# The start of a fused transformer block: the first weight matrix in half-width pieces, x tiles in another place among the loads

## The chip, the cores and the metric

The kernel runs on one core of a Trainium2 chip. The metric is device time in microseconds (us) of one execution. "Fast" runs are those that show no slow state. A ratio is the mean time of one kernel's fast runs over the mean of the other's fast runs of the same rounds, so it is not quite the ratio of the medians that are quoted.

Engines: PE is the tensor engine, PEld its weight loads, DVE the vector engine, ACT the scalar engine, POOL GpSimd, SP the sync engine, whose queue issues most DMAs. "LN1" is the first layer norm. A load "lands" when its data are in on-chip memory; it then counts up a semaphore, on which the reader waits. "Eviction" is the copy of a finished sum out of PSUM, the memory that PE writes to.

## The reference, cut to what matters

```python
# x: [1, 2048, 1024] bf16, D = 1024
h  = x + attention(layernorm(x) @ wqkv) @ wo     # sliding, dilated window of 8, 32 heads
h2 = h + mixer(layernorm(h))                     # gated MLP with a 2048 x 2048 token mix
```

Only the first step matters here: `layernorm(x) @ wq` for the first four tiles of 128 rows. `wq` is 1024 x 1024, 2 MB in bf16.

## The kernel before

PE runs 12 warm-up matmuls on zeros. Meanwhile the first loads are issued on two queues, SP (`dma`) and ACT (`A.dma_start`):

```python
csb = cpool.tile([P, 416], BF16, name="csb")        # identity and small constants
dma_w(csb[:], consts_d.ap()[:, :])                  # POOL queue
...
x_slot(0)
dma(xts[0][0:64, :], x2d[0:64, :])                  # x tile 0 in two row halves
A.dma_start(xts[0][64:P, :], x2d[64:P, :])
x_slot(1)
...
for q, kt in ((dma, 0), (A.dma_start, 1), (dma, 2), (A.dma_start, None), (dma, 4),
              (A.dma_start, 3), (dma, 5), (dma, 6), (dma, 7)):
    if kt is None:
        q(xts[1], x2d[P:2 * P, :])                  # x tile 1
    else:
        q(wsb[0][:, kt, :], wq_view[:, kt, 0:D])    # one row block of wq, 256 KB
load_x(2); load_x(3)
dma(wsb[1][:], ...)                                 # wk, 2 MB
... x tiles 4 to 7, then wv, 2 MB
```

LN1 of a tile is `stats` (DVE), a root (ACT), a reciprocal and a normalising pass (DVE). PE then transposes the tile and multiplies it:

```python
ln(0); xpose(0, xns[0], (0, 2)); xpose(0, xns[0], (2, 5))
for i in range(TPC):                                # four tiles
    acc = new_acc()
    for kt in range(KT):                            # eight row blocks
        if kt == 2 and i == 0:
            xpose(0, xns[0], (5, KT)); ln(1)
        if kt == QSPLIT and i + 1 < TPC:            # QSPLIT = 5
            xpose(i + 1, xns[i + 1], (0, 4), (4, KT))
        for nh in range(2):                         # two column halves
            T.matmul(acc[:, nh, :], xnT[...kt...], wsb[0][:, kt, nh * CH:(nh + 1) * CH], ...)
    if i + 2 < TPC:
        ln(i + 2)
    A.copy(qs0[:, i], acc...)                       # eviction on ACT
```

Much later one load matters for an experiment: `dma(bB[:], B_b_sp.unsqueeze(0).to_broadcast([P, S]))`, a bias for the last stage.

Of the kernel before, what the change touches and what calls it, by code (L numbers as in the profile page):

```python
# [18 lines left out]
S, D, H, DH, W_WIN, DIL = 2048, 1024, 32, 32, 8, 2  # L19
F, FH = 3584, 1792  # L20
P = 128
NT = S // P
CH = 512
NCH = S // CH
TPC = CH // P
KT = D // P
# [3 lines left out]
EPS = 1e-5  # L30
SCALE = DH ** -0.5
NEG = -1.0e9
NWARM = 12
XRB = 4
QSPLIT = 5
POOLLAT = 2.2
# [7 lines left out]
def _consts():  # L44
    c = np.zeros((P, 128 + 32 + 128 + 128), np.float32)
    c[:, 0:128] = np.eye(P)
    for p in range(P):
        c[p, 128 + p // 4] = 1.0
    for k in range(P):
        h = k % 32  # L50
        c[k, 160 + 4 * h:160 + 4 * h + 4] = 1.0
    for w in range(W_WIN):
        for s in range(16):
            if s - DIL * w < 0:
                c[0:32, 288 + w * 16 + s] = NEG
    return c.astype(ml_dtypes.bfloat16)
# [81 lines left out]
def kernel(  # L138
# [13 lines left out]
    V, A, T = nc.vector, nc.scalar, nc.tensor  # L152
    dma = nc.sync.dma_start
    dma_w = nc.gpsimd.dma_start
    x2d = A_x[0]
    out2d = out[0]

    consts_d = nc.inline_tensor(_consts(), name="qt_consts")
# [7 lines left out]

    cpool = ctx.enter_context(tc.tile_pool(name="consts", bufs=1))
    csb = cpool.tile([P, 416], BF16, name="csb")
    dma_w(csb[:], consts_d.ap()[:, :])
    ident = csb[:, 0:128]  # L170
    E32 = csb[:, 128:160]
    B4 = csb[:, 160:288]
# [10 lines left out]
    def wtile(shape, name, tag):  # L183
        return w16.tile(shape, BF16, name=name, tag=tag)
# [6 lines left out]
    def new_acc():  # L191
        return ps_acc.tile([P, 2, CH], FP32, name="acc", tag="acc")
# [9 lines left out]
    wq_view = A_wqkv.rearrange("(kt p) n -> p kt n", p=P)  # L202
    xnT = {}
    xts = {}
    pairs = {}

    def x_slot(i):
        if i // 2 not in pairs:
            pairs[i // 2] = l1.tile([P, 2, D], BF16, name="xp", tag="x4k", bufs=4)
        xts[i] = pairs[i // 2][:, i % 2, :]  # L210

    def load_x(i):
        x_slot(i)
        dma(xts[i], x2d[i * P:(i + 1) * P, :])
# [5 lines left out]
    wps = ps_att.tile([P, CH], FP32, name="wps", tag="L")  # L220
    for _ in range(NWARM):
        T.matmul(wps[:], warm[:, 0:P], warm[:], start=True, stop=True)

    x_slot(0)
    dma(xts[0][0:64, :], x2d[0:64, :])
    A.dma_start(xts[0][64:P, :], x2d[64:P, :])  # L226
    x_slot(1)
    wsb = [wtile([P, KT, D], "wq", "wA"), wtile([P, KT, D], "wk", "wA"), wtile([P, KT, D], "wv", "wB")]
    for q, kt in ((dma, 0), (A.dma_start, 1), (dma, 2), (A.dma_start, None), (dma, 4), (A.dma_start, 3), (dma, 5), (dma, 6), (dma, 7)):
        if kt is None:  # L230
            q(xts[1], x2d[P:2 * P, :])
        else:
            q(wsb[0][:, kt, :], wq_view[:, kt, 0:D])  # L233
    load_x(2)
    load_x(3)
    dma(wsb[1][:], wq_view[:, :, D:2 * D])
    for i in range(TPC, 2 * TPC):
        load_x(i)
# [2 lines left out]
    def stats(i):  # L241
        st = l1.tile([P, 2, 6], FP32, name="bnst", tag="bnst")
        V.bn_stats(st[:, 0, :], xts[i][:, 0:512])  # L243
        V.bn_stats(st[:, 1, :], xts[i][:, 512:1024])  # L244
        V.bn_aggr(mv1[:, i, :], st[:])

    def rstd_of(i):
        sd = l1.tile([P, 1], FP32, name="sd1", tag="sd1")
        A.activation(sd[:], mv1[:, i:i + 1, 1], ACTF.Sqrt, bias=eps_t[:])
        V.reciprocal(rstd1[:, i:i + 1], sd[:])  # L250

    def norm(i):
        xn = l1.tile([P, D], BF16, name="xn", tag="xn", bufs=4)
        for n0, n1 in ((0, 256), (256, 640), (640, D)) if i == 0 else ((0, D),):
            V.tensor_scalar(xn[:, n0:n1], xts[i][:, n0:n1], mv1[:, i, 0:1], rstd1[:, i:i + 1], op0=ALU.subtract, op1=ALU.mult)  # L255
        return xn
# [5 lines left out]
    def xpose(i, xn, *parts):  # L262
        for k0, k1 in parts:
            if i not in tps or k0 == 2:
                tps[i] = (ps_acc if i or k0 else ps_att).tile([P, KT, P], BF16, name="tpa" if i or k0 else "tp0", tag="acc" if i or k0 else "L")
            for a in range(k0, k1):
                T.transpose(tps[i][:, a, :], xn[:, a * P:(a + 1) * P], ident)  # L267
        for k0, k1 in parts:
            A.copy(xnT[0][:, k0:k1, i * P:(i + 1) * P], tps[i][:, k0:k1, :])
# [16 lines left out]
    with tc.manual_schedule(engines=manual):  # L286
        wsq = l1.tile([P, 1], FP32, name="wsq", tag="wsq")
        A.activation(wsq[:], eps_t[:], ACTF.Sqrt)
        xns = {}

        def ln(i):
            stats(i)
            rstd_of(i)
            xns[i] = norm(i)

        ln(0)
        xpose(0, xns[0], (0, 2))
        xpose(0, xns[0], (2, 5))
        for i in range(TPC):
            acc = new_acc()  # L300
            for kt in range(KT):
                if kt == 2 and i == 0:
                    xpose(0, xns[0], (5, KT))
                    ln(1)
                if kt == QSPLIT and i + 1 < TPC:
                    xpose(i + 1, xns[i + 1], (0, 4), (4, KT))
                for nh in range(2):
                    T.matmul(acc[:, nh, :], xnT[0][:, kt, i * P:(i + 1) * P], wsb[0][:, kt, nh * CH:(nh + 1) * CH],  # L308
                             start=(kt == 0), stop=(kt == KT - 1))
            if i + 2 < TPC:  # L310
                ln(i + 2)
            if i == 0:
                qs0 = att.tile([P, TPC, DLO, P], BF16, name="qs0", tag="oT")
            A.copy(qs0[:, i], acc[:].rearrange("p a b -> p (a b)").rearrange("p (m dl) -> p dl m", dl=DLO))
            nc.sync.dma_start_transpose(att_in[0][0][:, :, i * P:(i + 1) * P], qs0[:, i])
    wo_sb = wtile([P, DLO, D], "wo_sb", "wB")
    win_view = B_w_in.rearrange("(kt p) n -> p kt n", p=P)
# [537 lines left out]
    for c in range(NCH):  # L855
        wspT = wspTs[c]
        zg = p2.tile([P, NF, CH], BF16, name="zg", tag="zg")
        for fp in range(NF // 2):
            z1c = p2.tile([P, 2, CH], BF16, name="z1c", tag="z1c", bufs=8)
            dma(z1c[:], z1_d[2 * fp:2 * fp + 2, :, c * CH:(c + 1) * CH].rearrange("f p s -> p f s"))  # L860
            acc = new_acc()
            for j in range(2):
                f = 2 * fp + j
                for a in range(NT):
                    m_ = T.matmul(acc[:, j, :], z2sb[a][:, f * P:(f + 1) * P], wspT[:, a, :],  # L865
                                  start=(a == 0), stop=(a == NT - 1))
# [8 lines left out]
        for il in range(TPC):  # L875
            i = c * TPC + il
# [4 lines left out]
            for n0, n1 in cuts:  # L881
                acc = new_acc()[:].rearrange("p a b -> p (a b)")
                for f in range(NF):
                    wt, f0 = (wout_a, f) if f < 8 else (wout_b, f - 8)
                    for m0 in range(n0, n1, CH):
                        m1 = min(m0 + CH, n1)
                        T.matmul(acc[:, m0 - n0:m1 - n0], zg[:, f, il * P:(il + 1) * P], wt[:, f0, m0:m1],  # L887
                                 start=(f == 0), stop=(f == NF - 1))
# [29 lines left out]
```

## Time and profile before

| | before |
|---|---|
| median of the first three runs | 725.31 us (724.75 to 726.04) |
| span of the profiled execution | 723.8 us |
| PE busy | 714.0 us |
| transposes of x tile 2 start | 15.43 us |
| first matmul with wk | 24.52 us |

The page of the kernel before, parts 1 and 4: busy time by engine, and the chain of work that ended last, by engine.

```profile
PE 714.0 (99%) x3392; PEld 364.1 (50%) x3454; DVE 413.0 (57%) x435; ACT 238.2 (33%) x302; POOL 49.6 (7%) x57
...
PE 98%; DMA 1%; issue 0%; DVE 0%; ACTq 0%; ACT 0%
```

The profiled execution took 725.55 us (span 723.8).

PE is the limit everywhere but at the edges. The waits of PE over the whole run of the kernel before (who waited for whom: us in total, times, longest):

```profile
PE wps L222 <- DVE warm L219: 1.3, 1, 1.3
PE acc L308 <- DMA wq<-in_A_wqkv_dram: 1.1, 1, 1.1
PE tpa L267 <- DVE xn L255: 0.6, 1, 0.6
```

All three lie in the first 12 us. The timeline of PE there, kernel before: start, duration, line, operation, count, and in brackets the idle time before it with what ended it. L308 are the matmuls with wq, L267 the transposes, L396 the matmuls with wk.

```profile
7.16 1.04 PE L308 MATMUL acc<-wq,xnT 128*128 128x512 bf16 x4
...
8.20 0.59 PE L308 MATMUL acc<-wq,xnT 128*128 128x512 bf16 x2
9.86 1.02 PE L308 MATMUL acc<-wq,xnT 128*128 128x512 bf16 x4 [1.07 <-DMA wq<-in_A_wqkv_dram]
11.52 0.62 PE L267 MATMUL tpa<-csb,xn 128*128 128x128 bf16 x8 [0.63 <-DVE xn L255]
11.97 3.62 PE L308 MATMUL acc<-wq,xnT 128*128 128x512 bf16 x15
15.43 0.61 PE L267 MATMUL tpa<-csb,xn 128*128 128x128 bf16 x8
...
24.52 0.81 PE L396 MATMUL acc<-xnT,wk 128*128 128x512 bf16 x3
```

Up to 11.52 PE waits for a piece of wq, then for LN1 of x tile 1. From there it has no hole. So the start of tile 2's transposes (15.43) and of wk (24.52) are the marks for what the start is worth.

The loads under it, kernel before: issue, and the landing of the first and the last of the 16 parts of each load, one for each DMA engine. This table is made from the trace's landing records.

```
load              queue  issued  first part  last part
wq piece 0        SP      1.41      4.56       5.84
x tile 1          ACT     2.29      6.58       8.80
wq piece 3        ACT     2.76      8.37       9.82
wq piece 7 (last) SP      7.46     10.30      11.49
x tile 2          SP      7.83     10.96      12.15
```

Piece 3, on the ACT queue, landed after piece 4 on SP (9.13), though PE uses it first. Piece 7 was issued late: SP waited 2.2 us for a semaphore that an earlier load held until 7.44. The last parts of pieces 6 and 7 and of x tile 2 land 0.66 us apart (10.83, 11.49, 12.15), like other loads of 256 KB.

### The profile page before, as it was taken

Reading aid. Unit: us, or ns where it says so; the run is one execution under the profiler, and the core shown is the slowest. Engines: PE = TensorE matmul, PEld = TensorE weight load, DVE = VectorE, ACT = ScalarE, POOL = GpSimd, SP = SyncE. Lnnn points to the kernel's source line nnn. Section 1 sums busy time; section 2 is a strip of 40 time slices with the busy share of each in tenths; the row PEclk is TensorE's granted clock in tenths of the full one; section 3 lists DMA queues with packets and bytes.
Section 4 is the critical chain, followed back from the end, with each engine's and each line's share of the span. In section 5 each row is a group of like instructions: output and inputs, shape, how many; then the busy total and the mean of one; then the engine's idle time right before and its main releaser. Section 6 shows DMA issues by size and latency. Waiting matters only on the chain.

```text
span 723.8 us, 8387 instructions
## 1 busy us (share of the span) xinstructions
PE 714.0 (99%) x3392; PEld 364.1 (50%) x3454; DVE 413.0 (57%) x435; ACT 238.2 (33%) x302; POOL 49.6 (7%) x57
## 2 busy tenths in 40 slices
PE   8999999999999999999999999999999999999998
PEld 3666665666644444445445444444444444444444
DVE  5698999989998999876970202222222222222222
ACT  4389452632346785776735520000000000000000
POOL 0011200111002102000113000000000000000000
PEclk9999999999999999999999999999999999999999
DMA  8996564567664842651339978453115311120001
GB/s 300 265 314 126 193 174 148 159 211 257 211 256 145 212 169 75 228 140 69 140 113 257 255 195 294 158 141 120 31 43 139 119 34 44 36 89 8 1 19 69
DMA packets 119442, 107.74 MB, mean 149 GB/s; under 512 B 72588, under 2 KB 97452, under 8 KB 119404
## 3 DMA queue, kind: packets, MB, share of 16 engines
q1 hardware_dynamic: 110208, 73.35, 34.9%
q0 software_dynamic: 7760, 32.03, 12.9%
q10 hardware_dynamic: 1436, 1.84, 0.8%
q8 instruction: 27, 0.44, 0.3%
q14 instruction: 11, 0.09, 0.0%
HBM read 58.76 MB, written 31.65 MB: 125 GB/s over the span
## 4 chain that ended last, share of the span: by engine, by line
PE 98%; DMA 1%; issue 0%; DVE 0%; ACTq 0%; ACT 0%
PE acc L865 27%; PE acc L396 21%; PE acc L758 13%; PE acc L887 13%; PE acc L708 13%; PE acc L643 8%; PE acc L308 2%; DMA xp<-in_A_x_dram 1%; PE L L491 1%; PE tpa L267 0%; ACTq L233 0%; DVE bnst L243 0%; ACTq L226 0%; DVE bnst L244 0%; DVE xn L255 0%
## 5 line engine op out<-in xcount | busy, mean ns | idle before, releaser
L452 DVE TENSOR_TENSOR prod<-qT,kT 128x4096 bf16<-128x4096 bf16 (+1 forms) x36 | 73.1, 2048 | 4.0 <-DMA qT<-qs_220 3.8
L708 PEld LDWEIGHTS <-hnT 128*128 128x128 bf16 x512 | 50.1, 98 | 47.1
L887 PEld LDWEIGHTS <-zg 128*128 128x128 bf16 x462 | 45.2, 98 | 51.7
L586 DVE TENSOR_TENSOR prod<-vT,AB 128x4096 bf16<-128x4096 bf16 (+1 forms) x31 | 64.2, 2083 | 0.7
L588 DVE TENSOR_TENSOR oT<-oT,prod 128x4096 bf16<-128x4096 bf16 (+1 forms) x31 | 64.4, 2079 | 0.1
L889 DVE TENSOR_TENSOR ot<-acc,hr 128x1024 bf16<-128x1024 f32 (+2 forms) x18 | 19.9, 1106 | 73.1 <-PE acc L887 64.2
L887 PE MATMUL acc<-wout_a,zg 128*128 128x512 bf16 (+1 forms) x260 | 58.0, 372 | 0.3
L708 PE MATMUL acc<-win_1461,hnT 128*128 128x512 bf16 x248 | 57.6, 379 | 0.4
L396 PE MATMUL acc<-xnT,wk 128*128 128x512 bf16 x253 | 56.4, 379 | 0.3
L758 PE MATMUL acc<-hnT,win_1661 128*128 128x512 bf16 x256 | 56.2, 379 | 0.0
L396 PE MATMUL acc<-xnT,wv 128*128 128x512 bf16 x250 | 55.6, 379 | 0.3
L643 PE MATMUL acc<-wo_sb,oT 128*128 128x512 bf16 x249 | 55.4, 379 | 0.3
L407 ACT CAST stg<-acc 128x1024 bf16<-128x1024 f32 x36 | 36.4, 1011 | 57.7 <-PE acc L396 47.1
L396 PEld LDWEIGHTS <-wk 128*128 128x128 bf16 x256 | 36.8, 145 | 18.7 <-issue 0.7
L396 PEld LDWEIGHTS <-wv 128*128 128x128 bf16 x256 | 37.0, 145 | 18.2
L708 PE MATMUL acc<-win_1556,hnT 128*128 128x512 bf16 (+1 forms) x252 | 44.0, 325 | 0.2
L887 PE MATMUL acc<-wout_b,zg 128*128 128x512 bf16 (+1 forms) x193 | 43.8, 372 | 0.2
L758 PE MATMUL acc<-hnT,win_1667 128*128 128x512 bf16 x192 | 42.4, 379 | 0.0
L396 PE MATMUL acc<-xnT,wq 128*128 128x512 bf16 x187 | 41.7, 379 | 0.2
L715 ACT ACTIVATE u<-acc 128x1024 bf16<-128x1024 f32 (+1 forms) x32 | 29.4, 918 | 34.6 <-PE acc L708 34.6
L643 PEld LDWEIGHTS <-oT 128*128 128x128 bf16 x256 | 25.0, 98 | 30.2
L758 PEld LDWEIGHTS <-win_1661 128*128 128x128 bf16 x256 | 25.0, 98 | 29.9 <-issue 0.4
(271 smaller groups left out, 945.2 us busy)
## 6 DMA issues: line engine op xcount, KB each, us to landing
z_d<-z1s SPq DMA_DIRECT2D x28, 256.0 KB, 2.8
z1c<-z_d SPq DMA_DIRECT2D x28, 256.0 KB, 2.7
z_d<-u SPq DMA_DIRECT2D x12, 448.0 KB, 2.5
xr<-in_A_x_dram SPq DMA_DIRECT2D x16, 256.0 KB, 3.0
h_d<-hb SPq DMA_DIRECT2D x16, 256.0 KB, 2.0
hr<-h_d SPq DMA_DIRECT2D x16, 256.0 KB, 2.8
out_dram<-ot SPq DMA_DIRECT2D x15, 256.0 KB
xp<-in_A_x_dram SPq DMA_DIRECT2D x14, 256.0 KB, 5.5
```

The lines of the kernel that those rows point to most:

```text
L396: G["mmins", c, xi, dp] = T.matmul(G[key][:, j, :], wv[:, kt, dl, :], xnT[c][:, kt, :], start=(kt == 0), stop=(kt == KT - 1))
L407: A.copy(stg[:], G[key][:])
L452: V.tensor_tensor(qs[w]["prod"][:, d0:d1], qT[:, d0:d1], kT[:, d0:d1, o:o + CH], op=ALU.mult)
L586: V.tensor_tensor(dst[:, :, sq].rearrange("p d (q s) -> p d q s", q=nq), vv, abb, op=ALU.mult)
L588: V.tensor_tensor(oTs[c][:, :, sq], oTs[c][:, :, sq], pvs[w, q0][:, :, sq], op=ALU.add)
L643: T.matmul(st["acc", il][:, nh, :], oTs[c][:, dl, il * P:(il + 1) * P], wo_sb[:, dl, nh * CH:(nh + 1) * CH], start=(dl == 0), stop=(dl == ...
L708: T.matmul(accf[:, n0:n1], hnTs[c][:, il, kt, :], wins[hf][:, kt, n0:n1], start=(kt == 0), stop=(kt == KT - 1))
L715: A.activation(st["u", il][:, hf * 1024:hf * 1024 + wd], G["accz", c, il, hf][:].rearrange("p a b -> p (a b)")[:, 0:wd], ACTF.Gelu_apprx_t ...
L758: T.matmul(G["accy", c, fp][:, j, :].rearrange("p (a b) -> p a b", a=TPC), wt[:, kt, f0 * P:(f0 + 1) * P], hnTs[c][:, :, kt, :], start=(kt ...
L865: m_ = T.matmul(acc[:, j, :], z2sb[a][:, f * P:(f + 1) * P], wspT[:, a, :], start=(a == 0), stop=(a == NT - 1))
L887: T.matmul(acc[:, m0 - n0:m1 - n0], zg[:, f, il * P:(il + 1) * P], wt[:, f0, m0:m1], start=(f == 0), stop=(f == NF - 1))
L889: V.tensor_tensor(ot[:, n0:n1], acc[:, 0:n1 - n0], hr[:, n0:n1], op=ALU.add)
```

## The change

The intent is to give PE work with the first half of wq while the second is on its way, and to have x tile 1 early. Loads are cut into larger pieces of half width (1 KB rows), all wq goes on one queue, tile 0 runs through all row blocks of one column half and then of the other, and the LN1 of tile 2 moves behind the eviction of tile 0.

```diff
-NWARM = 12
+NWARM = 11
-    dma_w(csb[:], consts_d.ap()[:, :])
+    dma_w(csb[:, 0:128], consts_d.ap()[:, 0:128])
...
-    (the loop over (queue, kt) above)
+    def wq_part(nh, k0, k1):
+        dma(wsb[0][:, k0:k1, nh * CH:(nh + 1) * CH], wq_view[:, k0:k1, nh * CH:(nh + 1) * CH])
+    dma(xts[0][:, 0:CH], x2d[0:P, 0:CH])
+    A.dma_start(xts[0][:, CH:D], x2d[0:P, CH:D])
+    A.dma_start(xts[1], x2d[P:2 * P, :])
+    wq_part(0, 0, 4)
+    wq_part(0, 4, KT)
+    wq_part(1, 0, 4)
     load_x(2)
+    wq_part(1, 4, KT)
     load_x(3)
+    dma(csb[:, 128:416], consts_d.ap()[:, 128:416])
...
-        xpose(0, xns[0], (0, 2))
-        xpose(0, xns[0], (2, 5))
+        for part in ((0, 2), (2, 5), (5, KT)):
+            xpose(0, xns[0], part)
+        ln(1)
         for i in range(TPC):
             acc = new_acc()
-            for kt in range(KT):
-                ... (as above)
+            for n, (nh, kt) in enumerate([(nh, kt) for nh in range(2) for kt in range(KT)] if i == 0
+                                         else [(nh, kt) for kt in range(KT) for nh in range(2)]):
+                if n == (12 if i == 0 else 2 * QSPLIT) and i + 1 < TPC:
+                    xpose(i + 1, xns[i + 1], (0, 4), (4, KT))
+                T.matmul(... one half ...)
-            if i + 2 < TPC:
+            if i + 2 < TPC and i:
                 ln(i + 2)
             A.copy(qs0[:, i], ...)
+            if i == 0:
+                ln(2)
```

More of the change, by code (lines that the diff above doesn't have):

```diff
@@ L224 @@
     x_slot(0)
-    dma(xts[0][0:64, :], x2d[0:64, :])
-    A.dma_start(xts[0][64:P, :], x2d[64:P, :])
     x_slot(1)
     wsb = [wtile([P, KT, D], "wq", "wA"), wtile([P, KT, D], "wk", "wA"), wtile([P, KT, D], "wv", "wB")]
-    for q, kt in ((dma, 0), (A.dma_start, 1), (dma, 2), (A.dma_start, None), (dma, 4), (A.dma_start, 3), (dma, 5), (dma, 6), (dma, 7)):
-        if kt is None:
-            q(xts[1], x2d[P:2 * P, :])
-        else:
-            q(wsb[0][:, kt, :], wq_view[:, kt, 0:D])
+    def wq_part(nh, k0, k1):
[6 more added lines that the diff above has]
+    wq_part(1, 0, 4)
     load_x(2)
+    wq_part(1, 4, KT)
     load_x(3)
+    dma(csb[:, 128:416], consts_d.ap()[:, 128:416])
     dma(wsb[1][:], wq_view[:, :, D:2 * D])
@@ L296 @@
         ln(0)
-        xpose(0, xns[0], (0, 2))
-        xpose(0, xns[0], (2, 5))
+        for part in ((0, 2), (2, 5), (5, KT)):
+            xpose(0, xns[0], part)
+        ln(1)
         for i in range(TPC):
             acc = new_acc()
-            for kt in range(KT):
-                if kt == 2 and i == 0:
-                    xpose(0, xns[0], (5, KT))
-                    ln(1)
-                if kt == QSPLIT and i + 1 < TPC:
+            for n, (nh, kt) in enumerate([(nh, kt) for nh in range(2) for kt in range(KT)] if i == 0 else [(nh, kt) for kt in range(KT) for nh in range(2)]):
+                if n == (12 if i == 0 else 2 * QSPLIT) and i + 1 < TPC:
                     xpose(i + 1, xns[i + 1], (0, 4), (4, KT))
-                for nh in range(2):
-                    T.matmul(acc[:, nh, :], xnT[0][:, kt, i * P:(i + 1) * P], wsb[0][:, kt, nh * CH:(nh + 1) * CH],
-                             start=(kt == 0), stop=(kt == KT - 1))
-            if i + 2 < TPC:
+                T.matmul(acc[:, nh, :], xnT[0][:, kt, i * P:(i + 1) * P], wsb[0][:, kt, nh * CH:(nh + 1) * CH],
+                         start=(kt == 0), stop=(kt == KT - 1))
+            if i + 2 < TPC and i:
                 ln(i + 2)
```

## The prediction

> **What bounds the kernel.** The tensor engine: the page gives PE 714.0 of 723.8 us busy (99%), and the chain that ended last is PE for 98%. In the wait view PE waits only three times: 1.3 us for the warm-up tile, 1.1 us for a piece of wq, 0.6 us for the normalised second x tile. So only the first 12 us hold anything to win. The timeline there: first useful matmul at 7.16; a hole from 8.8 to 9.86 (wq piece 3, landed 9.82), one from 10.9 to 11.52 (x tile 1 landed at 8.80, its LN1 ended at 11.47). From 11.52 PE is without a hole: matmuls take 0.216 us, tile 0 is done near 11.97 + 6 x 0.216 = 13.27, and the transposes of tile 2 start at 15.43.
>
> **What the change does.**
> - x tile 0 arrives by column halves: the first statistics need one half (3.4), not both (3.9). Off the path, since weights come later.
> - x tile 1 is second on the ACT queue, lands near 5.5 to 6, and its LN1 is done near 9.6: the 0.6 us hole goes.
> - Tile 0 uses the left half of wq first, so arrival and use run in the same order: the 1.1 us hole goes as such.
> - Against that: the last four matmuls of tile 0 now wait for the fourth wq piece, behind x tile 2. Bytes up to its end: three x tiles 0.79 MB, identity 0.03, wq 2.10, together 2.92 MB. Before, the DMA records reach that sum at 10.9 us, and landings lag by about 1.15 (wq complete at 11.49). And wq moves in 1 KB packets: in this trace those take 46 ns, 2 KB ones 84, so 9% more time on 2.1 MB, about 0.45 us. The Trainium skill ("DMA: Bandwidth & Descriptors", Specifications) puts line rate at 512 B and up; the trace says a little is still lost at 1 KB. Estimate: fourth piece lands at 12.3 (11.6 to 12.8), tile 0 done at 13.2.
> - LN1 of tile 2 moves behind the eviction of tile 0 on ACT. Eviction starts 0.2 after the tile's end, takes 0.99, then root to normalised tile takes 1.08: transposes of tile 2 no earlier than 2.34 after tile 0's end, against 2.16 that PE needs for ten matmuls: a new hole near 0.2 us.
>
> **Sum on the path.** Tile 2's transposes start at about 12.3 + 0.9 + 2.34 = 15.5, against 15.43. Two holes are swapped for two others; the start stays bound by bytes. If pieces come faster than I think, up to 0.7 us is won; I allow 0.3. Everything later follows PE. The load queue starves less (before, 233 to 340 GB/s from 10.5 to 13.5), so wk lands about 1 us earlier (19.3 before), and DVE's attention starts about 1 us earlier (32.85 before). PE does not need these.
>
> **Predicted time:** 724.9 us, range 723.8 to 726.0; faster by over 2% 0.01, within 2% 0.98, slower by over 2% 0.01.
>
> **What would show it.** x tile 1's statistics near 7; PE holes at the first wq pieces (7 to 12) ending on wq landings; the fourth piece near 12.3; tile 2's transposes between 14.8 and 15.9 after a short wait for the normalised tile; wk's first matmul within 0.7 us of 24.5; PE gapless after that.
>
> **What would make it wrong.** Pieces of wq landing over 0.7 us off the byte sum (the first loads run at 230 to 340 GB/s for reasons the trace does not show); PE waiting for wk near 24; or an altered order of later DMA that delays attention.

## The result, and the profile after

| | before | after |
|---|---|---|
| median, first comparison | 725.17 us (4 runs) | 724.12 us (4 runs, 723.90 to 724.44) |
| span of the profiled execution | 723.8 | 722.3 |
| transposes of x tile 2 start | 15.43 | 14.32 |
| first matmul with wk | 24.52 | 23.43 |
| PE's last weight load to the end | 3.70 | 3.35 |

The ratio is 0.9984 with a 95% interval of 0.9967 to 1.0002: within 2%, and not clear of noise in this first comparison.

The page of the kernel after, parts 1 and 4:

```profile
PE 716.2 (99%) x3453; PEld 364.1 (50%) x3453; DVE 412.7 (57%) x435; ACT 238.0 (33%) x302; POOL 49.2 (7%) x57
...
PE 98%; DMA 1%; SPq 0%; DVE 0%; issue 0%
```

Its PE is still the limit. The busy time is no measure of the gain: it rose by 2 us, in part because the trace of before lacks some matmul records (3392 against 3453).

The waits of PE in the kernel after:

```profile
PE wps L222 <- DVE warm L219: 1.3, 1, 1.3
PE tp_157 L272 <- DVE xn L260: 0.7, 1, 0.7
PE acc L310 <- DMA wq<-in_A_wqkv_dram: 0.6, 1, 0.6
PE tpa L272 <- ACT xnT L274: 0.6, 1, 0.6
```

The timeline of PE in the kernel after, same columns (L310 are the matmuls with wq, L272 the transposes, L400 those with wk):

```profile
7.21 0.33 PE L272 MATMUL tpa<-csb,xn 128*128 128x128 bf16 x3 [0.57 <-ACT xnT L274]
7.37 2.75 PE L310 MATMUL acc<-wq,xnT 128*128 128x512 bf16 x12
9.96 0.61 PE L272 MATMUL tpa<-csb,xn 128*128 128x128 bf16 x8
11.22 3.18 PE L310 MATMUL acc<-wq,xnT 128*128 128x512 bf16 x14 [0.65 <-DMA wq<-in_A_wqkv_dram]
14.32 0.62 PE L272 MATMUL tpa<-csb,xn 128*128 128x128 bf16 x8
...
23.43 1.89 PE L400 MATMUL acc<-xnT,wk 128*128 128x512 bf16 x8
```

Twelve matmuls now run without a hole, the transposes of x tile 1 follow at once (its LN1 is long done), and only the fourth piece of wq is waited for. The loads of the kernel after, from the landing records:

```
load              queue  issued  first part  last part
wq piece 1        SP      1.19      5.83       6.15
x tile 1          ACT     1.19      4.97       5.28
wq piece 2        SP      1.66      7.22       7.50
wq piece 3        SP      2.20      8.71       8.98
x tile 2          SP      2.75      9.39       9.69
wq piece 4 (last) SP      3.32     10.89      11.18
```

Two things stand out beside the earlier landings. x tile 1 lands at 5.28 in place of 8.80. And all 16 parts of a load land within 0.3 us, where before they were spread over 1.2 to 2.2 us.

**Where the 1.45 us of span went.** I lined up the weight loads of PE from the end of both traces. From 29 us to the last one the distance between the kernels is 1.10 us, constant to 0.01. So the start is worth 1.10 us in this pair of executions, and PE passes it on whole. That is not the typical worth, since the profiled execution of before is a slow one: the medians differ by 1.05 us, or 0.79 in e0, and without the 0.35 us of the end that leaves 0.4 to 0.7 us for the start. A second trace of the old start, e11, reaches wk at 23.89, only 0.46 us behind after. The other 0.35 us lie behind PE's last instruction. There SP goes through a list of waits on semaphores, in order of their numbers. From the traces' records of SP (the time at which each wait was passed):

```
before: last store uses semaphore 110, landed 722.55
  722.56 wait 110   722.62 wait 111   722.68 wait 113   722.75 wait 114   722.80 wait 115   722.87 wait 116
after:  last store uses semaphore 117, landed 721.41
  720.41 wait 110   ...   720.66 wait 116   721.42 wait 117
```

Each wait takes 0.06 us even when long fulfilled. Eight semaphores go round over the DMAs of the SP and ACT queues. The change issues three such DMAs fewer, so the last store happens to take the last semaphore of the list, and the rest of the list is passed while the store is under way.

### The profile page after: what moved, and what is told of

Its sections match the earlier page's. It is cut to its first block, busy times and chain, and to the rows that moved or that the text cites. A ratio compares the mean times of both kernels' runs of the same rounds, so it can differ in the third digit from the quotient of the medians.

```text
span 722.3 us, 8442 instructions
## 1 busy us (share of the span) xinstructions
PE 716.2 (99%) x3453; PEld 364.1 (50%) x3453; DVE 412.7 (57%) x435; ACT 238.0 (33%) x302; POOL 49.2 (7%) x57
## 4 chain that ended last, share of the span: by engine, by line
PE 98%; DMA 1%; SPq 0%; DVE 0%; issue 0%
PE acc L869 27%; PE acc L400 21%; PE acc L762 13%; PE acc L712 13%; PE acc L891 13%; PE acc L647 8%; PE acc L310 2%; DMA wq<-in_A_wqkv_dram 1%; PE L L495 1%; SPq L229 0%; PE tpa L272 0%; SPq L214 0%; DVE ot L893 0%; SPq L231 0%; PE pb L567 0%
## 5 line engine op out<-in xcount | busy, mean ns | idle before, releaser
L400 PE MATMUL acc<-xnT,wk 128*128 128x512 bf16 x256 | 56.5, 379 | 0.0
L400 PE MATMUL acc<-xnT,wv 128*128 128x512 bf16 x256 | 55.9, 379 | 0.0
L400 PEld LDWEIGHTS <-wk 128*128 128x128 bf16 x256 | 36.8, 145 | 18.7 <-issue 0.7
L400 PEld LDWEIGHTS <-wv 128*128 128x128 bf16 x256 | 37.0, 144 | 18.3
L400 PE MATMUL acc<-xnT,wq 128*128 128x512 bf16 x192 | 42.1, 379 | 0.0
```

The source lines that it names most:

```text
L400: G["mmins", c, xi, dp] = T.matmul(G[key][:, j, :], wv[:, kt, dl, :], xnT[c][:, kt, :], start=(kt == 0), stop=(kt == KT - 1))
```

## The experiments

Theory after reading: (X) x tile 1 early takes its LN1 off the path; (R) wq on one queue, in order of use, lands earlier and together; (E) the end of the program gains 0.35 us from the semaphore that the last store takes. Rivals: (H) it is the half-width pieces and the order of the halves; and that two queues do no harm. One more rival was not tested by itself: the change also makes the wq loads larger (512 KB in place of 256), cuts x tile 0 by columns in place of rows, and loads 32 KB of constants first in place of 104. e0 to e4 ran on one chip, e5, e6, e8 and e9 on a second, e10 to e13 on a third. Times stand against runs of the kernel before in the same rounds; "the changed kernel" is e0. Each profile is of one of the timed executions.

### e0: the changed kernel again

> The changed kernel again, as the baseline of the runs beside it. Both theories: 0.8 to 1.5 us faster than before (ratio 0.998 to 0.999), fourth wq piece landing at 11.2 +- 0.2 us, transposes of x tile 2 at 14.3, first matmul with wk at 23.4.

724.09 us (724.01 to 724.35), before 724.88; ratio 0.9989 (0.9976 to 1.0002). Fourth piece at 11.17, transposes of tile 2 at 14.31, wk at 23.42, all as expected. The first comparison's 1.05 us is here 0.79, and again it is not clear of noise by its interval. Over all rounds the two hardly overlap: all nine runs of the changed kernel took at most 724.44 us, and 31 of 33 runs of the kernel before took more.

### e1: full-width pieces, old matmul order (Q and R against H)

```diff
-    def wq_part(nh, k0, k1):      # half width
+    def wq_part(k0, k1):          # full width, 2 row blocks each
+        dma(wsb[0][:, k0:k1, :], wq_view[:, k0:k1, 0:D])
-    for n, (nh, kt) in enumerate([... halves one behind the other ...] if i == 0 else [...]):
+    for n, (nh, kt) in enumerate([(nh, kt) for kt in range(KT) for nh in range(2)]):
```

> The changed kernel, but wq in four full-width pieces of two rows of blocks each (2 KB packets), and tile 0's matmuls in the old order (both halves for each block). Theory Q (the gain comes from the queues: all of wq on one queue in order of use, x tile 1 early on the other; halves are incidental): the fourth piece lands no later than 11.2, more likely 10.6 to 11.0 because 2 KB packets are a little quicker per byte; time equal to the changed kernel or up to 0.5 us faster. Rival H (the half-width pieces and the halves one behind the other are what helps): the fourth piece lands at 11.5 or later and the time goes back to that of the kernel before, within 0.3 us.

723.88 us (723.70 to 724.07), ratio 0.9985 (0.9971 to 0.9999). The fourth piece landed at 10.97, tile 2's transposes began at 14.22. H falls: without half widths and without the new order of halves the whole gain is there, and 0.2 us more. Nor is it needed that the parts land together: x tile 1 and the first piece are spread over 1.4 to 1.5 us here. e1 keeps the size of the loads (512 KB), the cut of x tile 0 and the short load of constants, so it says nothing of these. From x tile 2 to the fourth piece the landings are 1.37 us apart, against 1.48 in e0: 512 KB in 1 KB rows cost 8% more than in 2 KB rows.

### e2: pieces 2 and 4 on the ACT queue (R)

```diff
     def wq_part(nh, k0, k1):
-        dma(
+        (A.dma_start if k0 else dma)(
```

> The changed kernel, with the second and fourth wq pieces issued on the ACT queue behind x tile 1. Theory R (two queues with loads in flight at once spread the landing of one load over the 16 engines, 2 us from first to last in the kernel before against 0.3 in the changed one): the 16 part landings of the first three pieces spread over more than 1 us, the last needed piece lands at 11.7 or later, time 0.4 to 1 us above the changed kernel. Rival S (mixing is harmless; the old kernel's early loads were slow because of small pieces and SP blocked on semaphores): spreads stay near 0.3 us, last piece within 0.3 us of 11.2, time within 0.3 us of the changed kernel.

727.10 us (726.30 to 727.29), ratio 1.0028: slower than before. PE's waits in e2:

```profile
PE acc L310 <- DMA wq<-in_A_wqkv_dram: 3.2, 2, 1.9
PE wps L222 <- DVE warm L219: 1.3, 1, 1.3
```

and the place of the last wait in its timeline of PE:

```profile
14.22 3.18 PE L310 MATMUL acc<-wq,xnT 128*128 128x512 bf16 x14 [1.30 <-DMA wq<-in_A_wqkv_dram]
```

The fourth piece was issued at 2.22 and landed at 14.18, while x tile 3, issued on SP at 3.57, landed at 11.05. So in the changed kernel a second queue for wq does harm, but I had mis-sized it: I expected the spread over engines to cost 0.4 to 1 us (the spread was 0.6 to 1.5), and the larger cost is that the urgent load shares the engines with loads that nobody waits for yet. The 16 matmuls' last release came 3.01 us later than in e0 (14.22 against 11.21), and the time rose by 3.01: a hole at the start is paid in full. This does not show that two queues were what slowed the kernel before (see e5).

### e4: LN1 of tile 2 ahead of the eviction again

```diff
-            if i + 2 < TPC and i:
+            if i + 2 < TPC:
                 ln(i + 2)
...
-            if i == 0:
-                ln(2)
```

> The changed kernel, with the LN1 of x tile 2 back ahead of the eviction of tile 0 on ACT. If the hole of 0.4 us before the transposes of tile 2 comes from that order, the transposes start at 13.9 to 14.0 in place of 14.3 and the kernel is 0.3 to 0.4 us faster than the changed one. Rival: x tile 2's statistics come too late on DVE for it, then the eviction is held up and the time stays the same or grows by 0.2.

724.07 us (723.86 to 724.29): no different from e0. From the last release of PE to tile 2's transposes it is 14.05 - 11.04 = 3.01 us here and 14.31 - 11.21 = 3.10 in e0. The hole that this order makes is 0.09 us. I had read 0.4 from the weight loads' idle time; the matmuls themselves fill nearly all of it (14 x 0.216 = 3.02). A miss.

### e5, e8, e9: the kernel before, with only the first loads reordered

```diff
 e5   (A.dma_start, None), (dma, 0), (dma, 1), ... (dma, 7)                  # one queue, x tile 1 early
 e8   (dma, 0), (A.dma_start, None), (dma, 2), (A.dma_start, 1), (dma, 4), (A.dma_start, 3), ...  # two queues, early
 e9   (dma, 0), ... (dma, 4), (dma, None), (dma, 5), (dma, 6), (dma, 7)      # one queue, x tile 1 late
```

> The kernel before, with only the order of its first loads changed: all eight full-width wq pieces on the SP queue, x tile 1 alone on the ACT queue ahead of everything but x tile 0. Theory: two things make the gain, x tile 1 early (X) and one queue for wq (R). Both are here, so the gain should be there without half-width pieces or any new order on PE: x tile 1 lands by 6.5, last wq piece by 11.0, x tile 2 by 11.6, transposes of x tile 2 near 14.3 to 14.6, time 0.7 to 1.2 us below before. Rival (the order of tile 0's matmuls or the split identity load matter): less than 0.3 us below before.

> The kernel before, with x tile 1 moved one place forward on the ACT queue, ahead of wq piece 1; the two queues still share wq. X alone: x tile 1 lands near 7.0 in place of 8.80, the 0.6 us hole before its transposes goes; last wq piece (11.5) and x tile 2 (12.15) land as before, and the LN1 of x tile 2 (landing + 2.7 us) then sets the transposes of tile 2 at 14.9 or so: about 0.5 us below before. If only the single queue matters: within 0.2 us of before.

> The kernel before, with all wq pieces on the SP queue and x tile 1 there too, behind piece 4, so that it is still late. R alone: landings spread less over the engines (under 1 us from first to last), x tile 1 lands near 8.4 to 8.8, last wq piece near 10.9; PE still waits for x tile 1's LN1 (near 11.2); transposes of tile 2 near 15.0 to 15.3, 0.2 to 0.5 us below before. If x tile 1's place is all: within 0.2 us of before.

Before had 724.90 in these rounds (724.31 to 727.39).

- e5: 724.78 (724.33 to 725.18), ratio 0.9991 (0.9975 to 1.0007). That is 0.12 below before, where I had expected 0.7 to 1.2 and had given the rival less than 0.3: a miss. In its profile x tile 1 landed at 6.71, the last wq piece at 11.20, and x tile 2 only at 11.87; tile 2's transposes waited for its LN1 and began at 14.65, wk at 23.76. That is 0.76 earlier than in the slow profile of before, but only 0.13 earlier than in e11, which has the old start whole. Nor did one queue land the loads earlier: in e11, with two, the last wq piece came at 11.10 and x tile 2 at 11.79. So X and R on the old pieces do not give the gain. The end of e5 is still the old one (3.68 us behind PE's last load).

```profile
14.65 0.62 PE L267 MATMUL tpa<-csb,xn 128*128 128x128 bf16 x8 [0.46 <-DVE xn L255]
...
23.76 2.54 PE L396 MATMUL acc<-xnT,wk 128*128 128x512 bf16 x11
```

- e8: 726.66, but in two groups, 724.07 and 724.67 against four runs at 726.62 to 726.97. The profile shows one of the slower group: x tile 1 at 7.59, but the first wq piece on ACT at 9.11 and parts of one load up to 2.75 us apart. What I expected of X holds for the times of the two quick executions only, of which there is no trace.
- e9: 726.92 (725.98 to 728.47), ratio 1.0024: slower, where I had expected a little faster. x tile 1 landed at 9.24, not at 8.4 to 8.8, and PE waited for its LN1:

```profile
PE tpa L267 <- DVE xn L255: 1.9, 1, 1.9
...
11.96 0.62 PE L267 MATMUL tpa<-csb,xn 128*128 128x128 bf16 x8 [1.92 <-DVE xn L255]
```

(a line of e9's waits and one of its timeline; the profile is of the quickest of its six executions). So one queue with x tile 1 late is worth nothing: LN1 needs 2.7 us from the landing (9.24 to 11.96), and that must be hidden.

### e13: the changed kernel with x tile 1 late (X)

```diff
-    A.dma_start(xts[1], x2d[P:2 * P, :])
...
     wq_part(1, 0, 4)
+    dma(xts[1], x2d[P:2 * P, :])
     load_x(2)
```

> The changed kernel, with x tile 1 issued late: on the SP queue behind the third wq piece. If its early landing (5.3) is the larger part of the gain at the start, it lands near 9.1 here, its LN1 ends near 11.8, PE waits for that, tile 0 ends near 13.1 and the transposes of tile 2 start near 15.3, 0.9 to 1.0 us later than in the changed kernel, and the time rises by the same. If wq's landing is what counts and x tile 1 is incidental: transposes of tile 2 within 0.3 us of 14.3.

725.37 us (725.06 to 727.84), before 725.03. That is 0.34 above before, where e0 was 0.79 below: x tile 1's place is worth about 1.1 us in the changed kernel, a little over the 0.9 to 1.0 expected (the two stand on different chips, each against its own before). The profiled execution was the slowest of the five; in it one of 16 parts of each load landed 1.1 us behind the others, x tile 1 was complete at 10.48, and PE waited 2.36 us for its LN1:

```profile
13.20 1.03 PE L272 MATMUL tpa<-csb,xn 128*128 128x128 bf16 x8 [2.36 <-DVE xn L260]
```

### e6: the fourth piece ahead of x tile 2

```diff
-    load_x(2)
     wq_part(1, 4, KT)
+    load_x(2)
```

> The changed kernel, with the fourth wq piece issued ahead of x tile 2. The changed kernel's PE waits for that piece at 11.2; a 256 KB load takes 0.66 to 0.7 us of the queue, so the piece should land at 10.5, tile 0 end at 11.4, and the transposes of tile 2 start near 13.7 (eviction, then root, as measured: tile end + 2.3): 0.5 to 0.6 us below the changed kernel, near 723.5. Rival: x tile 2, now landing at 11.2, holds its LN1 up so that the transposes stay at 14.2 or later: less than 0.2 us.

723.82 us (723.61 to 724.76), ratio 0.9982 (0.9967 to 0.9997). About 0.3 us better than e0, on another chip; half of what I expected. The profile was taken of the slowest execution (span 723.0), so it doesn't show the order at its best: in it 15 of the 16 parts of the fourth piece landed by 10.33, and the last at 11.52.

### e10 and e11: the semaphore of the last store (E)

```diff
-    dma(bB[:], B_b_sp.unsqueeze(0).to_broadcast([P, S]))
+    for s0 in range(0, S, 1024):                # e10, on the changed kernel; 384 in e11, on the kernel before
+        s1 = min(s0 + 1024, S)
+        dma(bB[:, s0:s1], B_b_sp[s0:s1].unsqueeze(0).to_broadcast([P, s1 - s0]))
```

> The changed kernel, with the load of the bias (in the last stage) in two pieces instead of one: one more DMA, so every later DMA takes the next of the eight semaphores. Theory E (the end): the SP queue ends with a fixed list of waits, about 0.06 us each; in the changed kernel the last store's semaphore is the last of the list, here it becomes an early one, and the remaining waits come after its landing: about 0.4 us slower, with the first 25 us and PE's whole course unchanged. Rival (the 0.35 us between PE's last instruction and the end, that before has and the changed kernel has not, is a different cause): time within 0.1 us of the changed kernel.

> The kernel before, with the load of the bias in six pieces: five more DMAs, which bring the last store's semaphore to the end of the list of waits at the end, as in the changed kernel. Theory E: from the first matmul with wk to the end of the span 698.9 in place of 699.24 us, whatever the start does; time about 0.3 us below before, less clear because the start varies by about 1 us from run to run. Rival: 699.2 as before.

| kernel | semaphore of the last store | PE's last weight load to the end |
|---|---|---|
| before | 110 | 3.70 us |
| e11 (before, five more DMAs) | 116 | 3.34 us |
| after | 117 | 3.35 us |
| e10 (after, one more DMA) | 107 | 3.76 us |

The list runs from 107 to 116 before and to 117 after, so e11 ends on its last and e10 near its first. The span shows E plainly: e10 gives 0.41 us back, e11 wins 0.36 (its span from wk's first matmul, 23.89 to 722.78, is 698.9 us). In time e10 is 724.54 (724.49 to 724.66), 0.49 below its before (725.03) where e0 was 0.79 below. e11 is 725.04 against 725.03, so its gain doesn't show in the times: the starts of the old order scatter too much. The trace of e11 is also a second, quicker execution of the old start:

```profile
14.79 0.61 PE L267 MATMUL tpa<-csb,xn 128*128 128x128 bf16 x8
...
23.89 2.32 PE L396 MATMUL acc<-xnT,wk 128*128 128x512 bf16 x10
```

### e12: what the runs point to, together

```diff
+    wq in full-width pieces and the old matmul order (e1), fourth piece ahead of x tile 2 (e6)
-            if i not in tps or k0 == 2:
+            if i not in tps or (i == 0 and k0 in (2, 5)):   # third part of tile 0's transposes: its own PSUM tile
```

> The changed kernel with what the runs point to: full-width wq pieces (2 KB packets), the fourth piece ahead of x tile 2, and the third part of tile 0's transposes in a PSUM tile of its own (it waited 0.6 us for the copy of the second part). Fourth piece near 10.4, tile 0 done near 11.3, transposes of tile 2 near 13.6 to 13.8, wk's first matmul near 22.8: 0.4 to 0.7 us below the changed kernel, near 723.5. Rival: the landing of x tile 2 or of the identity holds it, and it stays within 0.2 us of the changed kernel.

723.67 us (723.45 to 724.33), before 725.03; ratio 0.9981 (0.9968 to 0.9993). PE's timeline in e12:

```profile
7.34 2.76 PE L310 MATMUL acc<-wq,xnT 128*128 128x512 bf16 x12
9.94 0.61 PE L272 MATMUL tpa<-csb,xn 128*128 128x128 bf16 x8
10.38 3.19 PE L310 MATMUL acc<-wq,xnT 128*128 128x512 bf16 x13
13.69 0.62 PE L272 MATMUL tpa<-csb,xn 128*128 128x128 bf16 x8
...
22.80 3.40 PE L400 MATMUL acc<-xnT,wk 128*128 128x512 bf16 x15
```

The wait for the fourth piece is gone (landed 10.23) and so is the one for the copy (the 0.6 us behind ACT xnT in the waits of after). wk starts 0.63 us earlier than in the kernel after. By its median it beats the kernel before by 1.36 us and the changed one by 0.42, or 0.57 if each stands against its own before. Three things changed at once, so it doesn't say what each is worth.

## Why the prediction was right or wrong

"Within 2%" was right, and 724.12 lies in the range (723.8 to 726.0). The size of the gain was not: from 725.31 to 724.9, 0.4 us, was predicted, of which the sum itself gave nothing and the rest was an allowance. Measured were 1.05 us and, in e0, 0.79. That the time fell into the range is in part luck: one landing was wrong by 1.1 us, and 0.35 us came from the end, which the prediction did not look at.

- *"So only the first 12 us hold anything to win."* Nearly. PE's course was rigid from 29 us on, as predicted, but 0.35 us lay behind PE's last instruction (e10, e11). I had not looked there.
- *"x tile 1 ... lands near 5.5 to 6 ...: the 0.6 us hole goes."* Right: 5.28, LN1 ended at 9.1, no hole. e13 puts its worth near 1.1 us when it is taken away from the changed kernel; on the old pieces, with one queue too, it gave no clear gain (e5).
- *"fourth piece lands at 12.3 (11.6 to 12.8), tile 0 done at 13.2."* This is the step that failed: 11.18. Its terms: the DMA records of after reach 2.92 MB at 10.5 us, where I had 10.9 plus 0.45 for 1 KB packets; and the landing lags that sum by 0.7, where I had 1.15. The 9% for 1 KB packets was right (8% in steady flow, e1). What I took over wrongly was the pace and the lag of the old loads, from one slow execution: by 8 us they had moved 1.74 MB, after 2.02, and the parts of one load came up to 2.2 us apart. Why they were slower is not shown. Two queues for wq don't explain it: e11 has the old order and reaches 2.92 MB at 10.6, and e5, with one queue, at 10.7. The lag, found in the same way, is 1.0 to 1.1 us in both. The first packets start at 2.12 to 2.14 us in all five traces of the old pieces and at 1.77 to 1.79 in eight of nine of the new. e2 shows that pieces on the second queue cost 3.0 us in the new order.
- *"Two holes are swapped for two others."* Wrong as a sum for that reason. The second new hole, for the LN1 of tile 2, was predicted at 0.2 us and is 0.09 (e4).
- *"Tile 2's transposes between 14.8 and 15.9"* failed (14.32), and *"wk's first matmul within 0.7 us of 24.5"* too (23.43): both follow from the fourth piece. Tile 0 done plus 2.34 would have given 14.4.
- *"wk lands about 1 us earlier"*, and DVE's attention: right in direction. wk landed at 17.50 in place of 19.30, attention began at 31.58 in place of 32.85, and no time came of it.

The intent of the change, work with one half of wq while the other is under way, is not where the gain is (e1). Tile 0 needs all 2 MB in either order, and the pieces arrive in order of use in both.

What stays open: why one engine falls behind in some executions. A part that is late stays late for all later loads of the start, and the times of such executions are the slow ones of their kernel (e6, e13, the groups of e8). The old order showed it more: 724.3 to 727.4 in all its runs, against 723.9 to 724.4 in nine runs of the changed kernel. Between 2 and 9 us the trace of before has 40 packets of over 250 ns, that of after 10, but the records don't say which engine or why. Open too is what makes most of the gain at the start. Taken away singly from the changed kernel, X and R each cost over 1 us; added to the old pieces, singly or together (e5), neither gives a clear gain. e1, which shares the order of loads with the changed kernel and has larger pieces, column halves of x tile 0 and 32 KB of constants in front, gains 1.00 us, of which 0.35 is the end; e5 gains 0.12. By these medians, from two chips, about 0.5 us goes with these three (the rival for e5 names the load of constants), with the earlier transposes of tile 0, or with x tile 2, which landed at 9.60 in e1 and at 11.87 in e5. No run puts one of them alone on the old kernel.

## What to carry to other kernels

Where one engine is busy to the end, its first microseconds count in full, and there it matters when each load lands: in the changed kernel two pieces of wq on the second queue cost 3.0 us, and x tile 1, on which a chain of 2.7 us of LN1 hangs, cost 1.1 us when it came late. Don't predict a new load order from the pace of one execution of the old: two traces of the old start reach wk 0.64 us apart. And look behind the last instruction of the busy engine: a change in the number of DMAs moved the end by 0.35 us.

## What the Trainium skill lacked or had wrong

- "DMA: Bandwidth & Descriptors", Specifications, gives 512 B as the least transfer for line rate. Here 1 KB packets took 46 ns and 2 KB ones 84 in the trace of before, and 512 KB took 1.48 us in 1 KB rows against 1.37 in 2 KB rows (e0, e1): 1 KB rows still cost 8% more. Only this row of the page is meant.
- The same page, Issuing engines are not separate DMA queues, says that DMAs of several queues run on the same 16 engines and interleave. The runs agree, and show the price, which it doesn't name: two of four pieces on the second queue cost 3.0 us (e2), where x tile 3, issued on the other queue 1.35 us after the fourth piece, landed 3.1 us before it.
- The same page, Why a DMA increments its semaphore by 16 and not by 1, says that the engines of one load finish independently. It gives no size: 0.3 us from first to last part in the kernel after, up to 2.75 us in e8, and a lag of a single part of 1.2 us in e6.
- I found no page that says that the end of a program depends on which semaphore its last store uses: the waits are passed in fixed order, and its place among them is worth 0.35 to 0.42 us (e10, e11).
